# Softmax weights turned through DRAM: one write per block, two read-backs by head, and V of a pair in one transfer

## The chip, the cores and the metric

The kernel runs on one core of one Trainium2 chip. The metric is device time in microseconds (us). The kernel before has a median of 1463.87 us over 3 runs (1461.8 to 1474.76).

## What is computed

The reference is a thresholded attention followed by a bilinear feed-forward layer, all in 32-bit floats.

```python
batch, n_heads, seq, head_dim = (8, 8, 576, 64)
scores = scale * np.matmul(q, k.transpose(0, 1, 3, 2))
thresh = np.max(scores, axis=-1, keepdims=True) - tau
scores = np.where(scores >= thresh, scores, -1000000000.0)
scores = scores - np.max(scores, axis=-1, keepdims=True)
attn = np.exp(scores)
attn = attn / (np.sum(attn, axis=-1, keepdims=True) + 1e-09)
attn_out = np.matmul(attn, v)
# (B,H,S,D) -> (B*S, H*D), then with w_a, w_b (512 x 1536) and w_out (1536 x 512):
a = x @ w_a
b = x @ w_b
return a * b @ w_out
```

## The kernel before, in words

**Tiling.** Heads are taken in pairs (`pairs`, 32 of them, four to a batch). A pair's 576 queries are cut into four blocks of 128 and a tail of 64 (`units`, 160 in all; "block" below means one of them). A tile of weights `tw` has the queries on 128 partitions, and for each of the two heads 576 keys, kept as 18 groups of 32. In a tail both heads share the 128 partitions.

**One step of the main loop** (line 925, step g) issues, in this order: the scores of block g (`scores`, L352, on TensorE, PE); the turn of the weights of block g-1 (`turn_blocks`); the weighing of block g (`weigh`: maximum L359, exp L380, threshold L383); the product with V of a finished half of a pair (`weighted`, which calls `product`, L483); the read-back of block g-2 (`turn_back`); the normalising of block g (L402); loads of q, k and v for pairs some steps ahead (`load` L147, `load_v` L170); stores of finished output rows (L833). Between these, `advance` issues feed-forward matmuls (L633, L706, L763) in portions worked out from column counts, so that PE has other work while weights are prepared.

**The order of the work** is written out by hand: `keep_order` at the end ties every instruction to the one before it on its engine. So each queue does its list strictly in the order written, and an instruction that waits holds up everything behind it on that engine. All transfers of the main loop go through the queue of SyncE (SP). In one step it holds the writes of block g-1 (L457), the read-backs of block g-2 (L466 or L469), then the loads (L147, L170) and the stores.

**How weights are turned.** PV needs the keys on the partitions. VectorE (DVE) transposes each 32 x 32 square in place (L446); what is left is to move 32-partition groups of queries against groups of keys, and that is done through DRAM. `turn_blocks` writes the tile to the DRAM tile `swap` with four transfers, one for each group g of 32 partitions (L457). Each moves 4 pieces of 9 x 32 numbers (1152 bytes) per partition. `turn_back` reads `swap` into the tile `wT` (`turned_tile`, two buffers) with one transfer over 128 partitions (L466), again in pieces of 1152 bytes. For tails, `swap` has two planes, and the read-back of pairs 4 to 31 is two transfers (L469), into the fifth column of the two `wT` tiles of the pair's second half. The first eight blocks (`BY_PE`) are turned by PE instead and don't take this way.

In `wT` the partition is 64 times the head, plus 32 times the half c of the key groups, plus the key's place within its group; slot s (0 to 8) counts the groups in a half. V lies in the same way in `vm`: for pairs 4 to 31 (`HP` is 4) `load_v` issues four transfers, one for each head and half, to 32 partitions each (L170), with rows of 9 x 64 numbers (2304 bytes). Pairs 0 to 3 are loaded twice: at first by head (L172), and a second time (`again`) in the order that the turned weights need.

`product` multiplies slot by slot; within a slot it goes over the heads j, and each matmul reads the 64 partitions of head j:

```python
for s in range(NSLOT):
    for j in range(2):
        rows = slice(j * D, (j + 1) * D)
        for c in range(2):
            y = j ^ c
            nc.tensor.matmul(pv[c * D:(c + 1) * D, y], vm[rows, s], wT[y](rows, s),
```

A half of a pair is two blocks; for pairs 4 to 31 the second half also takes the tail. A block's read-back is issued at step g+2 and the product that uses it is written into step g+3 (`PV_LAG` is 3).

Of the kernel before, what the change touches and what calls it, by code (L numbers as in the profile page):

```python
# [10 lines left out]
FP32 = mybir.dt.float32  # L11
# [41 lines left out]
def kernel(  # L53
# [38 lines left out]
    nc = tc.nc  # L92
    B, H, S, D = q.shape
    P = 128
    Q = 32
    DM = H * D
    DFF = w_a.shape[1]
    HP = H // 2
    NT = 4
# [3 lines left out]
    NB = S // Q  # L103
    R = 96
    NR = S // R
    SH = S // 2
# [3 lines left out]
    NSLOT = 9  # L110
    G = P // Q
# [4 lines left out]
    def pool(name, bufs, **kw):  # L116
        return ctx.enter_context(tc.tile_pool(name=name, bufs=bufs, **kw))
# [5 lines left out]
    scratch = pool("scratch", 3, space=bass.MemoryType.DRAM)  # L123
# [9 lines left out]
    loaded = {}  # L133
# [24 lines left out]
    def load_v(i, again=False):  # L158
        b, hp = pairs[i]
        if not again:  # L160
            loaded[i]["v"] = loads.tile([P, NSLOT, D], FP32, tag="vm", bufs=HP, name="vm")
        for j in range(2):
            rows, half = v[b, 2 * hp + j], loaded[i]["v"][j * D:(j + 1) * D]
            if i >= HP or again:
                if i < HP:
                    rows = rows.rearrange("(c s p) d -> p c s d", c=2, p=Q)
                else:
                    rows = rows.rearrange("(p c s) d -> p c s d", c=2, p=Q)
                for c in range(2):
                    nc.sync.dma_start(half[c * Q:(c + 1) * Q], rows[:, c])  # L170
            else:
                nc.sync.dma_start(half, rows.rearrange("(s p) d -> p s d", p=D))  # L172

# [10 lines left out]
    for f in range(NG):  # L184
        for c in range(HP):
            for dst, w in ((wa_sb, w_a), (wb_sb, w_b)):
                src = []
                for r in range(2):
                    chunks = [(2 * c + e) % HP * 2 + (r + (c >= HP // 2)) % 2 for e in range(2)]
                    cols = slice(f * CW + r * CH, f * CW + (r + 1) * CH)  # L190
                    rows = w[:, cols].bitcast(U32).rearrange("(k p) f -> p k f", p=D)
# [89 lines left out]
    for _ in range(TW_BUFS):  # L281
        t = work.tile([P, 2 * NB, Q], FP32, tag="tw", bufs=TW_BUFS, name="rows")
# [10 lines left out]
    load_rows(2, "k", rooms[5])  # L293
    load_weights(RAWS)
    load_v(0)
    load_rows(3, "q", rooms[6])
    load_rows(3, "k", rooms[7])
# [15 lines left out]
    prepared, scored, weights, turned, whole = {}, {}, {}, {}, {}  # L313
    x_of, xtail_of = {}, {}
    blocks, complete, swaps = [], [], {}
# [97 lines left out]
    def turned_tile():  # L413
        return work.tile([P, G + 1, NSLOT, Q], FP32, tag="wT", bufs=2, name="wT")
# [17 lines left out]
    def part(i, u):  # L432

        if i < HP:
            return {1: (i, 0), 3: (i, 1), NT: (i, 2)}.get(u)
        return {1: (i, 0), NT: (i, 1)}.get(u)
# [4 lines left out]
    def turn_blocks(i, u):  # L441

        ws, _ = weights.pop((i, u))
        t = whole.pop((i, u))
        for w in ws:
            nc.vector.transpose(w, w)  # L446
        if u < NT:
            swap = scratch.tile([G, P, NSLOT * Q], FP32, tag="swap", name="swap")
        else:
            swap = scratch.tile([2, P, NSLOT * Q], FP32, tag="swapt", name="swap")  # L450
        swaps[i, u] = swap
        for g in range(G):
            if u < NT:
                to, n = swap[g], G
            else:
                to, n = swap[g % 2, (1 - g // 2) * D:(2 - g // 2) * D], 2
            nc.sync.dma_start(to.rearrange("(r p) e -> p r e", p=Q),  # L457
                              t[g * Q:(g + 1) * Q, 0:n * NSLOT].rearrange("p (r s) e -> p r (s e)", r=n))

    def turn_back(i, u):  # L460

        swap = swaps.pop((i, u)).rearrange("g p e -> p g e")
        if u < NT or i < HP:
            turned[i, u] = turned_tile()
            n = G if u < NT else 2
            nc.sync.dma_start(turned[i, u][:, 0:n].rearrange("p g s e -> p g (s e)"), swap)  # L466
        else:
            for y in range(2):
                nc.sync.dma_start(turned[i, 2 + y][:, G].rearrange("p s e -> p (s e)"), swap[:, y])  # L469

    def join(out, lo, hi):
        nc.scalar.copy(out, lo)
# [447 lines left out]
    n = 0  # L920
# [4 lines left out]
    for g in range(len(units) + PV_LAG):  # L925
# [4 lines left out]
        if here:  # L930
            i, u = units[g]
# [19 lines left out]
        if g > BY_PE and g <= len(units):  # L951
            turn_blocks(*units[g - 1])
# [14 lines left out]
        if g > BY_PE:  # L967
            advance(PORTIONS[1] * pace)
            n = g - PV_LAG
            if BY_PE <= n < len(units) and part(*units[n]):  # L970
                p, h = part(*units[n])
                if pairs[p][1] == 0:
                    make_x(2 if h == 1 and p >= HP and pairs[p][0] % GT == 0 else 1)
                make_room()
                weighted(*part(*units[n]))
                running["owed"] -= NSLOT * width(*part(*units[n])) // 2
            if BY_PE + 1 < g <= len(units) + 1:
                turn_back(*units[g - 2])
# [20 lines left out]
        for p in range(1, NPR):  # L999
            if g == first[p] - 1:  # L1000
                load_v(p)
        if BY_PE <= g < BY_PE + HP:
            load_v(g - BY_PE, again=True)
# [54 lines left out]
```

## Time and profile before

| | |
|---|---|
| median of 3 runs | 1463.87 us (1461.8 to 1474.76) |
| profiled execution: its time, its span | 1467.37 us, 1465.6 us |
| PE busy | 1387.9 us (95%) |
| DVE, ACT, POOL busy | 1014.9 us (69%), 682.9 us (47%), 479.5 us (33%) |
| chain that ended last: PE, DVE, DMA, SP's queue | 78%, 7%, 5%, 5% |
| SP's transfers (hardware_dynamic q1) | 217.73 MB, 60.7% of 16 engines' span |

The transfers that the change touches, from the list of DMA issues (KB of one, median us from issue to landing) and the tiles' medians of one issue:

| transfer | issues | KB each | us to landing | ns of one issue |
|---|---|---|---|---|
| swap<-tw, block (L457) | 480 | 144 | 2.6 | 433 |
| swap<-tw, tail (L457) | 128 | 72 | 2.0 | 433 |
| wT<-swap, block (L466) | 120 | 576 | 4.7 | 382 |
| wT<-swap, tail of pairs 0 to 3 (L466) | 4 | 288 | 3.3 | 382 |
| wT<-swap, tail of the others (L469) | 56 | 144 | 2.9 | 452 |
| vm<-in_v_dram (L170) | 128 | 72 | 3.3 | 422 |

How to read the lines below: an entry of the waits says which instruction waited (engine, output tile, line of the kernel), for what, how long in total, how often, and the longest. A line of the timeline gives start, duration, engine or queue ("SPq" is SP's queue), line, operation and tiles, and how many instructions are merged. "Issue" in the waits is time in which nothing that the profile shows was waited for. A table by stage gives, for each stretch, the length, then the busy time (and count) of PE, of its weight loads, of DVE, ACT and POOL, then the granted clock, the share of the DMA engines' time, and GB/s.

### The profile page before, as it was taken

To read this page: it belongs to the slowest core of one execution; us is meant where nothing else is said; L and a number is where in the kernel's file an instruction comes from. 1 tells how busy PE (TensorE), PEld (TensorE's weight loads), DVE (VectorE), ACT (ScalarE), POOL (GpSimd) and SP (SyncE) were. 2 spreads that over 40 slices of the span, in tenths; PEclk is the share of its full clock that TensorE was granted. 3 is DMA by queue.
4 is the path that set the end of the run, shared out by engine and by line. 5 is a ranking of instruction groups with operands and counts; after the bars stand their busy time and mean duration, and the time that the engine had idled before them with its cause. 6 is when DMAs were issued, how large, how long until landed. Compare 5 with 4: busy or idle time off the path is not lost.

```text
span 1465.6 us, 76332 instructions
## 1 busy us (share of the span) xinstructions
PE 1387.9 (95%) x34208; PEld 1248.2 (85%) x34208; DVE 1014.9 (69%) x2245; ACT 682.9 (47%) x1243; POOL 479.5 (33%) x668
## 2 busy tenths in 40 slices
PE   5788999999999999999999899999999999999998
PEld 4677687987989889899998788998898979989997
DVE  6898688787767787586757677767767776755223
ACT  5787455545545554454444445444545455431110
POOL 2774713423060606033334224150606060605000
PEclk9999999999999999999999999999999999999999
DMA  9976677668756775577555766477656776450000
GB/s 217 227 207 181 155 183 190 167 169 189 195 135 160 165 203 145 137 174 180 142 135 138 163 165 169 121 177 167 173 147 144 179 188 165 122 148 30 4 17 17
DMA packets 325080, 223.21 MB, mean 152 GB/s; under 512 B 169616, under 2 KB 308880, under 8 KB 324752
## 3 DMA queue, kind: packets, MB, share of 16 engines
q1 hardware_dynamic: 322384, 217.73, 60.7%
q8 instruction: 269, 4.41, 1.3%
q10 hardware_dynamic: 2368, 0.59, 0.2%
q14 instruction: 59, 0.48, 0.1%
HBM read 128.58 MB, written 89.65 MB: 149 GB/s over the span
## 4 chain that ended last, share of the span: by engine, by line
PE 78%; DVE 7%; DMA 5%; SPq 5%; issue 3%; ACT 1%; POOL 1%; ACTq 0%; DVEq 0%; POOLq 0%
PE pab L633 24%; PE pab L706 18%; PE po L763 17%; PE pv L483 9%; PE sc L352 9%; DMA wT<-swap 2%; SPq L457 2%; DVE mx L359 2%; SPq L147 1%; DMA qT<-in_q_dram 1%; DVE tw L446 1%; DVE tw L383 1%; PE po L809 1%; SPq L225 1%; POOL kept L732 0%
## 5 line engine op out<-in xcount | busy, mean ns | idle before, releaser
L402 ACT ACTIVATE tw<-tw,rcp 128x576 f32<-128x576 f32 x272 | 197.8, 769 | 216.9 <-DVE rcp L396 216.8
L359 DVE TENSOR_REDUCE mx<-sc 128x1 f32<-128x576 f32 x288 | 205.6, 751 | 134.6 <-PE sc L352 131.3
L380 ACT ACTIVATE tw<-sc,bias,scalars 128x576 f32<-128x576 f32 x288 | 239.3, 831 | 9.8 <-DMA vm<-in_v_dram 0.2
L599 POOL TENSOR_TENSOR h<-h,u 128x512 f32<-128x512 f32 x28 | 35.1, 1272 | 621.8 <-DVE h L676 485.8
L383 DVE SCALAR_TENSOR_TENSOR tw<-sc,thr,tw 128x576 f32<-128x576 f32 x288 | 223.0, 798 | 14.0 <-ACT tw L380 13.8
L763 PE MATMUL po<-wo_sb,h 64*64 64x256 f32 x3264 | 222.9, 377 | 0.0
L352 PE MATMUL sc<-kT,qT 64*64 64x288 f32 x2016 | 192.0, 405 | 10.5 <-ACT xt L490 4.7
L446 DVE STREAM_TRANSPOSE tw<-tw 128x576 f32<-128x576 f32 x272 | 196.0, 754 | 0.8 <-ACT tw L402 0.8
L483 PE MATMUL pv<-wT,vm 64*64 64x160 f32 (+3 forms) x5184 | 182.4, 275 | 14.3 <-DMA wT<-swap 8.0
L763 PEld LDWEIGHTS po<-wo_sb,h 64*64 64x64 f32 x3264 | 167.4, 133 | 24.9
L483 PEld LDWEIGHTS pv<-wT,vm 64*64 64x64 f32 x5184 | 166.2, 135 | 25.3 <-issue 10.4
L763 PE MATMUL po<-sums_u,h 64*64 64x256 f32 x2448 | 163.9, 376 | 1.6 <-DVE h L714 1.6
L732 POOL TENSOR_TENSOR h<-h 128x256 f32<-128x256 f32 x168 | 117.4, 728 | 114.6 <-PE po L763 100.5
L352 PEld LDWEIGHTS sc<-kT,qT 64*64 64x64 f32 x2016 | 115.1, 133 | 32.5 <-ACT xt L490 12.3
L763 PEld LDWEIGHTS po<-sums_u,h 64*64 64x64 f32 x2448 | 123.4, 133 | 20.7 <-DVE h L714 2.3
L633 PE MATMUL pab<-xU,wb_sb 64*64 64x128 f32 x4096 | 133.5, 270 | 0.2 <-issue 0.2
L379 ACT ACTIVATE bias<-mx,scalars 128x1 f32<-128x1 f32 x288 | 83.0, 288 | 100.6 <-DVE mx L359 100.5
L633 PEld LDWEIGHTS pab<-xU,wb_sb 64*64 64x64 f32 x4096 | 127.6, 133 | 2.6 <-issue 0.5
L491 DVE COPY xT<-pv 64x128 f32<-64x128 f32 (+1 forms) x136 | 38.1, 280 | 120.3 <-PE pv L483 119.1
L633 PE MATMUL pab<-xS,wa_sb 64*64 64x128 f32 x2048 | 110.8, 270 | 3.2 <-POOL xS L506 2.0
L490 ACT COPY xT<-pv 128x128 f32<-128x128 f32 (+1 forms) x68 | 17.6, 258 | 206.0 <-PE pv L483 205.9
L706 PE MATMUL pab<-xS,wb_sb 64*64 64x256 f32 (+1 forms) x1536 | 99.9, 359 | 2.9 <-issue 2.9
(137 smaller groups left out, 2429.0 us busy)
## 6 DMA issues: line engine op xcount, KB each, us to landing
swap<-tw SPq DMA_DIRECT2D x480, 144.0 KB, 2.6
wT<-swap SPq DMA_DIRECT2D x120, 576.0 KB, 4.7
vm<-in_v_dram SPq DMA_DIRECT2D x128, 72.0 KB, 3.3
swap<-tw SPq DMA_DIRECT2D x128, 72.0 KB, 2.0
kT<-in_k_dram SPq DMA_DIRECT2D x112, 72.0 KB, 4.3
wT<-swap SPq DMA_DIRECT2D x56, 144.0 KB, 2.9
out_dram<-kept SPq DMA_DIRECT2D x30, 256.0 KB, 4.0
qT<-in_q_dram SPq DMA_DIRECT2D x112, 40.0 KB, 4.5
```

The lines of the kernel that those rows point to most:

```text
L352: nc.tensor.matmul(sc[j if u < NT else 0][to, c], qT[r, q0:q0 + D], kT[r, c * SH:(c + 1) * SH], start=True, stop=True)
L359: nc.vector.tensor_reduce(mx[:, c], sc[j], axis=AX.XY, op=ALU.max)
L379: nc.scalar.activation(bias[:, j:j + 1], mx[:, j:j + 1], AF.Copy, scale=e_nscale)
L380: nc.scalar.activation(wb[j], sb[j], AF.Exp, bias=bias[:, j:j + 1], scale=e_scale)
L383: nc.vector.scalar_tensor_tensor(out=wv, in0=sb[j], scalar=thr[:, j:j + 1], in1=wv, op0=ALU.is_ge, op1=ALU.mult, accum_out=sums[:, j:j + 1])
L402: nc.scalar.activation(w, w, AF.Copy, scale=rcp[:, j:j + 1])
L446: nc.vector.transpose(w, w)
L483: nc.tensor.matmul(pv[c * D:(c + 1) * D, y], vm[rows, s], wT[y](rows, s), start=(s == 0), stop=(s == NSLOT - 1))
L633: nc.tensor.matmul(out[c * D:(c + 1) * D, r, f * P:(f + 1) * P], w[g][k][rows, w0:w0 + D], moving[k][rows], start=(fresh and k == 0 and f ...
L706: nc.tensor.matmul(pab[c * D:(c + 1) * D, r], w[rows, f // n, k, fs + c * D:fs + (c + 1) * D], moving, start=(k == 0), stop=(k == H - 1))
L732: (nc.vector if state["over"] else nc.gpsimd).tensor_tensor(*a, **kw)
L763: nc.tensor.matmul(po[c * D:(c + 1) * D, r, y], ht[rows, t0:t0 + D], other[rows, f], start=(f == 0), stop=(f == NF // 2 - 1))
```

## The change

Three things change, and nothing else.

1. `turn_blocks` writes a block in one transfer: 128 partitions, for each head one run of 576 numbers (2304 bytes). `swap` is now one plane of [128, 576] for each head; a tail is one plane.
2. `turn_back` reads back by head: for each head j one transfer to the 64 partitions of that head, in pieces of 288 numbers (1152 bytes). Two consecutive pieces of a DRAM row go to two neighbouring partitions. A tail of pairs 4 to 31 takes four transfers (two heads, two tiles), one of pairs 0 to 3 takes two.
3. The half c of the key groups is now the lowest bit of the partition and no longer its bit of value 32. So V of a pair, for pairs 4 to 31, is one transfer to 128 partitions with rows of 2304 bytes. The second load of pairs 0 to 3 still takes four transfers, now to every second partition.

```diff
@@ load_v
+        vm = loaded[i]["v"]
+        if i >= HP:
+            nc.sync.dma_start(vm, v[b, 2 * hp:2 * hp + 2].rearrange("j (p s) d -> (j p) s d", s=NSLOT))
+            return
         for j in range(2):
-            rows, half = v[b, 2 * hp + j], loaded[i]["v"][j * D:(j + 1) * D]
-            if i >= HP or again:
-                if i < HP:
-                    rows = rows.rearrange("(c s p) d -> p c s d", c=2, p=Q)
-                else:
-                    rows = rows.rearrange("(p c s) d -> p c s d", c=2, p=Q)
+            rows, half = v[b, 2 * hp + j], vm[j * D:(j + 1) * D]
+            if again:
                 for c in range(2):
-                    nc.sync.dma_start(half[c * Q:(c + 1) * Q], rows[:, c])
+                    nc.sync.dma_start(half[c::2], rows[c * SH:(c + 1) * SH].rearrange("(s p) d -> p s d", p=Q))
@@ turn_blocks
-        if u < NT:
-            swap = scratch.tile([G, P, NSLOT * Q], FP32, tag="swap", name="swap")
-        else:
-            swap = scratch.tile([2, P, NSLOT * Q], FP32, tag="swapt", name="swap")
+        n = len(ws)
+        swap = scratch.tile([n, P, 2 * NSLOT * Q], FP32, tag="swap" if n == 2 else "swapt", name="swap")
         swaps[i, u] = swap
-        for g in range(G):
-            if u < NT:
-                to, n = swap[g], G
-            else:
-                to, n = swap[g % 2, (1 - g // 2) * D:(2 - g // 2) * D], 2
-            nc.sync.dma_start(to.rearrange("(r p) e -> p r e", p=Q),
-                              t[g * Q:(g + 1) * Q, 0:n * NSLOT].rearrange("p (r s) e -> p r (s e)", r=n))
+        nc.sync.dma_start(swap.rearrange("j p e -> p j e"), t[:, 0:n * NB].rearrange("p (j n) e -> p j (n e)", j=n))
@@ turn_back
-        swap = swaps.pop((i, u)).rearrange("g p e -> p g e")
+        swap = swaps.pop((i, u))
         if u < NT or i < HP:
             turned[i, u] = turned_tile()
-            n = G if u < NT else 2
-            nc.sync.dma_start(turned[i, u][:, 0:n].rearrange("p g s e -> p g (s e)"), swap)
-        else:
+        for j in range(2):
+            rows = slice(j * D, (j + 1) * D)
+            if u < NT:
+                nc.sync.dma_start(turned[i, u][rows, 0:G].rearrange("p g s e -> p g (s e)"),
+                                  swap[j].rearrange("(g p) (c e) -> (p c) g e", g=G, c=2))
+                continue
+            back = swap[0, (1 - j) * D:(2 - j) * D].rearrange("(y p) (c e) -> (p c) y e", y=2, c=2)
+            if i < HP:
+                nc.sync.dma_start(turned[i, u][rows, 0:2].rearrange("p y s e -> p y (s e)"), back)
+                continue
             for y in range(2):
-                nc.sync.dma_start(turned[i, 2 + y][:, G].rearrange("p s e -> p (s e)"), swap[:, y])
+                nc.sync.dma_start(turned[i, 2 + y][rows, G].rearrange("p s e -> p (s e)"), back[:, y])
```

## The prediction

> **What bounds the kernel now.** First the stage table, for where TensorE (PE) has holes, since a change of transfers can win no more than those. Columns: stretch, length, busy time of each engine, granted clock, DMA share, GB/s.
>
> ```profile
> 0.00:120.00 120.00, 85.33 (x2148) 72.88 (x2152) 95.34 (x213) 83.86 (x170) 64.96 (x80) 0.96 0.95 223
> 120.00:1320.00 1200.00, 1162.76 (x28537) 1046.49 (x28533) 868.10 (x1940) 583.73 (x1048) 392.80 (x554) 1.00 0.66 162
> 1320.00:1440.00 120.00, 119.97 (x3180) 112.40 (x3176) 40.48 (x68) 13.16 (x22) 21.69 (x34) 1.00 0.04 14
> ```
>
> PE is idle for 37.2 us of the 1200 in which the changed transfers run (120 to 1320). After that PE is full with feed-forward work left over, so the end comes when PE has done its list: a microsecond of PE idle filled before 1320 brings the end forward by one, and a new one puts it back. The first 120 us use the changed path little: blocks 0 to 7 are turned on PE.
>
> Second, PE's waits in 120 to 1320: waited for, us in total, times, longest.
>
> ```profile
> PE pv L483 <- DMA wT<-swap: 8.0, 6, 2.7
> PE pab L633 <- issue: 7.8, 14, 1.9
> PE sc L352 <- ACT xt L490: 4.7, 4, 1.2
> PE sc L352 <- DVE xt L491: 3.2, 3, 1.1
> PE pv L483 <- issue: 2.6, 4, 1.0
> ```
>
> The largest named wait is the product with V (L483) for turned weights read back from DRAM: 8.0 us. So the changed path ends last only at a few places; elsewhere PE does not wait for it.
>
> Third, the queue of SyncE (SP) at one such place, and the chain of waits there.
>
> ```profile
> 205.45 3.74 SPq L457 DMA_DIRECT2D swap<-tw  x4
> 209.29 0.40 SPq L466 DMA_DIRECT2D wT<-swap  x1
> 209.79 2.08 SPq L147 DMA_DIRECT2D qT<-in_q_dram  x4
> 211.91 2.88 SPq L170 DMA_DIRECT2D vm<-in_v_dram  x4
> ...
> 209.29 5.17 DMA wT<-swap
> 214.46 0.04 issue
> 214.50 2.08 PE pv L483 x67
> ```
>
> The read-back of block g-2 stands in SP's queue behind the four writes of block g-1. They took 3.74 us to issue; without a hold-up they take 1.76. From the trace's landing records I paired 65 PV blocks with the last read-back each uses: in 8 it lands after PV has begun (6.5 us together), in 26 less than 1.0 us before PV or later, in 34 less than 1.5. That list prices a shift: every read-back landing 0.5 us sooner fills 3.5 us, 1.0 sooner 5.2, 1.5 sooner 6.5; 0.5 later opens 5.5 us, 1.0 later 15.0, 1.5 later 30.8.
>
> Fourth, the rate of each transfer when it is alone: a read-back (704.0 to 705.4) and the four writes of a block (707.9 to 709.6); the last columns are DMA share and GB/s.
>
> ```profile
> 704.00:705.40 1.40, 1.40 (x32) 1.40 (x28) 1.37 (x2) 1.08 (x3) 0.00 (x0) 1.00 0.93 329
> 707.90:709.60 1.70, 1.70 (x72) 1.70 (x65) 1.16 (x5) 0.47 (x1) 0.00 (x0) 1.00 0.96 216
> ```
>
> Same bytes, same 1152-byte pieces, DMA engines over 90% busy in both: 329 GB/s for one transfer over 128 partitions, 216 for four over 32 each.
>
> **What the Trainium skill says.** "SBUF — State Buffer", Door 1: The DMA port swizzle: the DMA side has 16 ports, partitions 0 to 31 reach 8, 0 to 63 the same 8, and only a transfer over all 128 reaches 16. The trace agrees for 32 against 128 (216 against 329 GB/s); it shows no large 64-partition transfer, so for those I rest on the page. "DMA: Bandwidth & Descriptors", Rules for kernel authors: two transfers to disjoint partition halves serialize. No run yet shows that; the change makes just such a pair. [...] Here a read-back with the queue to itself took 4.1 us to land, against 1.8 for 590 kB at 329 GB/s.
>
> **The change, part by part.**
>
> *Writes.* A block of two heads: four transfers of 144 KB become one of 576 KB over 128 partitions, in rows of 2304 bytes. 120 such blocks and 32 tails: 608 issues become 152. Issue by the tile's median (0.433 us): 1.76 us become about 0.45, so SP is free 1.3 us sooner. Moving time: 590 kB at 216 is 2.73 us; at 329 it is 1.80. The bounds are 1.80 and 2.73 (writes to DRAM need not run like reads); I take 1.80 on the port page. Nobody waits for a write itself: its reader is issued one step, about 8 us, later, against a landing of 2.6 us. It counts only as what fills the rings ahead of the read-back.
>
> *Read-backs.* One of 576 KB becomes two of 288 KB over 64 partitions: 124 + 56 issues become 248 + 112. Each further issue costs 0.38 to 0.45 us of SP. Moving time: 1.80 us at 329 becomes 2.73 at 216, if 64 partitions are as 32; bounds 1.80 and 2.73. PV alternates heads from one matmul to the next, so an early first half is worth nothing. PV now waits for two landings per tile and head pair in place of one; queued behind it on PE is everything, in written order.
>
> *The sum at a critical block*, from the place at 707: before, writes issued from 707.00, read-back issued at 708.92, landed 4.8 us later at 713.7. After: bytes flow about 1.0 us after the first issue (as at 707), writes 1.80, read-backs straight behind in the same rings (issued by 708.3, long before 709.8) 2.73, receipt about 0.6 (bytes of the lone read-back end at 705.4, its landing is at 706.0): 707.0 + 1.0 + 1.80 + 2.73 + 0.6 = 713.1. That is 0.6 us sooner. With both bounds good (1.80, 1.80) 1.5 sooner; with both bad (2.73, 2.73) 0.3 later. Where issues were held up, as at 209 (3.74 in place of 1.76), a further 1 to 2 us come, and these are the places where PE waits. By the list above, 0.6 sooner everywhere is 3.8 us, and with the hold-ups some 5; one fifth I take off, because a PE that starts PV sooner meets its next wait sooner (scores waiting for the PSUM copies, 4.7 + 3.2 us). **-4 us.**
>
> *Tails.* Four writes of 72 KB become one; two read-backs become four for 28 tails and one becomes two for 4. Last issue: 1.75 + 0.45 = 2.2 us after the start of the block's writes before, 0.45 + 3 x 0.45 = 1.8 after. 295 kB in halves: 1.4 us at 216 in place of 0.9. Together +0.1 us, nothing to the list.
>
> *V.* 28 pairs go from four transfers over 32 partitions to one over 128 (row length 2304 bytes as before), 84 issues x 0.422 = 35 us of SP off. It hides under SP's slack except where q, k and v come together (157 to 232, 302 to 378): there a v group holds SP for 1.8 to 3.8 us, and the next block's writes stand behind it. Between 0 and -3 us; I take -0.5, since most of it is in the hold-ups already counted. The four pairs whose V is loaded again keep four transfers each, only to every second partition: 0. K's order of keys within a row, the matmuls and their operands' sizes stay as they are: 0; their order in every queue is written out (the order of each engine is fixed at the end), so no work changes place.
>
> *Sum:* the profiled execution took 1467.37 us (span 1465.6); minus 4.5 it would be 1462.9. It lies 3.5 us above the median of the runs, 1463.87; from that median, **1459.4 us**.
>
> **Rivals.**
> *Hidden or given back.* PE's idle time at PV is filled but returns at the next scores or in the copies of PV's banks: -2 to +2 us, 1464. For: PE's other waits sum to more than this one. Against: after 1320 PE has no waits at all, so idle filled anywhere counts.
> *The half-port read-back takes the place of the issue wait (slower).* Place: PV behind L466. If the pair of halves needs more than it saves, landings come later, and more than half of all blocks have under 1.5 us to spare. It decides at 1.0 us later (15 us, 1%): writes and read-backs would have to need 6.1 us together in place of the 4.5 of my sum, which is writes no faster than now and read-backs at 175 GB/s. At 1.5 us later it is +31, some 1494; at 1.2 later about 1485. For: the skill's pages both speak against halves. Against: 216 GB/s is measured for transfers with as few ports, and the earlier issue is arithmetic.
> *SP's queue was worth more than PE's waits show (faster by over 1%).* The chain gives SP's queue 5% and wT's transfers 2%; with 360 fewer issues q, k and blocks all come sooner. It must fill 15 of the 37 us idle: about 1447. Against: of those 37 us only some 13 name a transfer or stand at PV.
> That the transfers do not become fewer or wider is excluded by the access patterns; how wide the rows are on the wire is not.
>
> **How the numbers follow.** Forecast 0.55 (own range 1455 to 1463), hidden 0.20, half-port 0.15, SP's queue 0.10. 1% is about what a measurement of this kernel can tell from no change; bounds 1449.2 and 1478.5. Faster 0.10 (the last rival), same 0.75 (forecast and hidden), slower 0.15. Range 1448 to 1477: both middle cases, the near part of each outer one.
>
> **What would show it.** Right: writes landing near 3.5 us at 0.4 us of issue; GB/s near 329 in them; halves near 216; the wait of PV for wT below 4 us. Wrong: that wait above 10 us, halves landing later than 6 us behind the writes' first issue, or a time outside the range with PE's idle time in 120 to 1320 unchanged.

## The result, and the profile after

The changed kernel takes 1478.2 us (median of 17 runs, 1471.76 to 1483.28), the kernel before, in the same comparison, 1467.05 us (17 runs, 1461.67 to 1474.76). The ratio is 1.007, interval 1.0052 to 1.0089: slower by 0.7%, where 1459.4 us was forecast, and about 1 us above the upper end of the range. The profiled execution of the changed kernel took 1477.18 us (span 1475.4), 9.8 us more span than before.

First the stage table of the changed kernel, in the columns of the one shown for before.

```profile
120.00:1320.00 1200.00, 1158.17 (x28333) 1046.29 (x28329) 866.83 (x1936) 582.48 (x1046) 392.90 (x554) 1.00 0.62 161
1320.00:1440.00 120.00, 118.38 (x3159) 99.54 (x3156) 40.84 (x69) 13.94 (x23) 21.70 (x34) 1.00 0.10 27
```

In 120 to 1320 PE is idle for 41.8 us instead of 37.2, and it gets through 204 matmuls fewer. Next, PE's waits in that stretch: waited for, us in total, times, longest.

```profile
PE pab L632 <- issue: 16.0, 19, 1.8
PE sc L352 <- ACT xt L489: 7.0, 6, 1.3
PE pab L705 <- issue: 3.5, 5, 1.3
PE pv L482 <- issue: 2.1, 3, 0.8
...
PE pv L482 <- DMA wT<-swap: 1.5, 2, 0.8
```

The wait of the product with V (PV) for turned weights fell from 8.0 to 1.5 us, as forecast. But the wait at the top has no name: 16.0 us of "issue" ahead of the first layer of the feed-forward (`pab`, L632, L633 before), where it was 7.8. The two rows of `pab` together hold 19.5 us.

The summed time from each matmul's start to the next, after 120 us and put down to the kind of the later one, shows what the waits alone do not (us, worked out from the start times in the trace):

| | `pab` | PV | scores | second layer | span |
|---|---|---|---|---|---|
| before | 705.2 | 162.3 | 144.1 | 327.7 | 1465.6 |
| after | 724.9 | 152.5 | 143.6 | 328.2 | 1475.4 |

PV gained 9.8 us; `pab`, which no edit touches and whose data no changed transfer carries, lost 19.7. The sum is the change of the span. So the question was not why the gain at PV failed to come, but what holds PE in the feed-forward.

The transfers themselves did what was forecast. The page's list of DMA issues (count, size, median us from issue to landing), and the queue of SyncE (SP) at the place shown for before at 205:

```profile
swap<-tw SPq DMA_DIRECT2D x120, 576.0 KB, 3.5
wT<-swap SPq DMA_DIRECT2D x240, 288.0 KB, 4.6
```

```profile
207.73 0.56 SPq L450 DMA_DIRECT2D swap<-tw  x1
208.39 1.51 SPq L460 DMA_DIRECT2D wT<-swap  x2
```

The write's issue takes 0.56 us there, where four held SP for 3.74. The rates of the write alone (702.7 to 704.4) and of the two half read-backs (708.8 to 711.2), in the last column:

```profile
702.70:704.40 1.70, 1.67 (x62) 1.43 (x56) 1.70 (x4) 0.00 (x0) 0.00 (x0) 1.00 0.91 343
708.80:711.20 2.40, 2.40 (x51) 2.40 (x45) 2.07 (x4) 2.08 (x5) 0.00 (x0) 1.00 0.95 234
```

**What else uses the DMA engines.** The page's list of queues has a second row, the same in both kernels:

```profile
q8 instruction: 269, 4.41, 1.3%
```

These are 269 packets of 16 KB. PE's 34208 matmuls and as many weight loads are 68416 instructions; divided by 256 that is 267. So they are PE's own instructions, one packet for every 256. "Runtime: NRT & Kernel Launch" of the Trainium skill, section Instruction fetch mechanics, says just this: an engine's instructions are streamed in 16 KiB blocks of 256 through a DMA queue of the sequencer. It adds that crossing a block is mostly hidden. The trace agrees on the block, not on "hidden". One place in the changed kernel, in order: PE's timeline, SP's timeline, and the DMA queues in 899.0 to 901.7.

```profile
899.99 0.40 PE L632 MATMUL pab<-xT,wa_sb 64*64 64x128 f32 x8
900.21 0.40 PE L632 MATMUL pab<-xS,wa_sb 64*64 64x128 f32 x8
901.69 0.38 PE L632 MATMUL pab<-xS,wa_sb 64*64 64x128 f32 x5 [1.08 <-issue]
```

```profile
899.04 0.38 SPq L450 DMA_DIRECT2D swap<-tw  x1
899.52 2.09 SPq L460 DMA_DIRECT2D wT<-swap  x2
```

```profile
q1 hardware_dynamic: 1091, 0.67, 90.8%
q8 instruction: 1, 0.02, 3.2%
```

PE stops in the middle of a run of equal matmuls. A write and two half read-backs have just been issued, data holds the engines for 90.8% of the window, and in it lies one instruction packet, which ended 1.27 us before PE went on. In these lines 8 matmuls take 0.22 us; with as many weight loads, a block of 256 instructions lasts some 3.5 us at that rate (an estimate), while 2.66 us passed from the start of this fetch until PE went on. To count such places I took PE's stalls (over 0.25 us from start to start, after 120 us) that end 1.1 to 1.75 us after the end of an instruction packet: 30 with 22.4 us before, 39 with 36.4 us after. Within `pab` they are 13.0 and 30.3 us; that is 17.3 of the 19.7 lost. Some of these are coincidence: windows of the same width at other distances hold 2.5 to 10.2 us.

A count by place leaves chance nearly out. If the fetch causes a stall, the stall must come at a fixed place in PE's stream. Number all of PE's records in the trace (matmuls, weight loads and those of its sequencer; 68897 before, 269.1 blocks of 256). Of the 104 stalls before, 21 end at the places 193 to 195 of a block, and 35 of the 120 after, where chance would put one or two. They hold 15.4 us before and 32.8 after, in `pab` 12.9 and 30.0; all other stalls in `pab` hold 9.4 and 10.5. So 17.1 of the 19.7 us stand at one place in the instruction stream, whatever the matmul there reads. Below, these are the stalls "at the seam".

How late a fetch starts, against its place in the stream (one every 256 instructions, the earliest of each run taken as zero): median 1.27 us before, 1.61 after; one in ten over 2.66 before, over 3.53 after.

### The profile page after: what moved, and what is told of

Read it like the earlier page. It is cut to its first block, busy times and chain, and to the rows that moved or that the text cites. A ratio compares the mean times of both kernels' runs of the same rounds, so it can differ in the third digit from the quotient of the medians.

```text
span 1475.4 us, 75468 instructions
## 1 busy us (share of the span) xinstructions
PE 1390.5 (94%) x34208; PEld 1240.3 (84%) x34208; DVE 1017.0 (69%) x2245; ACT 682.8 (46%) x1243; POOL 480.2 (33%) x668
## 4 chain that ended last, share of the span: by engine, by line
PE 84%; DVE 8%; issue 4%; DMA 2%; ACT 1%; POOL 1%; SPq 0%; DVEq 0%; ACTq 0%; POOLq 0%
PE pab L632 27%; PE po L762 19%; PE pab L705 18%; PE sc L352 10%; PE pv L482 9%; DVE mx L359 2%; DVE tw L383 1%; PE po L808 1%; DVE tw L446 1%; DMA wT<-swap 1%; POOL kept L731 1%; DVE low L260 0%; PE tp L427 0%; DVE xT L490 0%; DMA scalars<-in_tau_dram 0%
## 5 line engine op out<-in xcount | busy, mean ns | idle before, releaser
L383 DVE SCALAR_TENSOR_TENSOR tw<-sc,thr,tw 128x576 f32<-128x576 f32 x288 | 223.3, 798 | 15.0 <-ACT tw L380 14.7
L762 PE MATMUL po<-wo_sb,h 64*64 64x256 f32 x3264 | 218.4, 377 | 0.0
L352 PE MATMUL sc<-kT,qT 64*64 64x288 f32 x2016 | 192.1, 404 | 10.2 <-ACT xt L489 7.0
L762 PEld LDWEIGHTS po<-wo_sb,h 64*64 64x64 f32 x3264 | 163.3, 133 | 26.4
L482 PEld LDWEIGHTS pv<-wT,vm 64*64 64x64 f32 x5184 | 165.2, 134 | 16.8 <-issue 10.4
L762 PE MATMUL po<-sums_u,h 64*64 64x256 f32 x2448 | 160.9, 376 | 1.6 <-DVE h L713 1.6
L632 PE MATMUL pab<-xU,wb_sb 64*64 64x128 f32 x4096 | 133.2, 270 | 1.0 <-issue 1.0
L632 PEld LDWEIGHTS pab<-xU,wb_sb 64*64 64x64 f32 x4096 | 126.8, 133 | 4.5 <-issue 1.5
L632 PE MATMUL pab<-xS,wa_sb 64*64 64x128 f32 x2048 | 108.5, 271 | 5.9 <-issue 3.8
L489 ACT COPY xT<-pv 128x128 f32<-128x128 f32 (+1 forms) x68 | 17.6, 259 | 198.6 <-PE pv L482 198.6
```

Of the source, the lines that this page charges most:

```text
L352: nc.tensor.matmul(sc[j if u < NT else 0][to, c], qT[r, q0:q0 + D], kT[r, c * SH:(c + 1) * SH], start=True, stop=True)
L383: nc.vector.scalar_tensor_tensor(out=wv, in0=sb[j], scalar=thr[:, j:j + 1], in1=wv, op0=ALU.is_ge, op1=ALU.mult, accum_out=sums[:, j:j + 1])
L632: nc.tensor.matmul(out[c * D:(c + 1) * D, r, f * P:(f + 1) * P], w[g][k][rows, w0:w0 + D], moving[k][rows], start=(fresh and k == 0 and f ...
L762: nc.tensor.matmul(po[c * D:(c + 1) * D, r, y], ht[rows, t0:t0 + D], other[rows, f], start=(f == 0), stop=(f == NF // 2 - 1))
```

## The experiments

Theories. **Ports**: the halves, at 64 partitions, move at a lower rate and come late at PV (the rival of the forecast). **SP**: the longer or more frequent issues hold something up. **Fetch**: long transfers keep the DMA engines from PE's next instructions. The expectations use letters, and call `pab` feed-forward. H, W and V name the part of the change that keeps the fetches waiting: the half read-backs, the one long write, or V with the longer rows. L says that a transfer does it by its length; D that the bytes ahead of the fetch do it, however they are cut. P stands in `e7` for the ports, against I for the second transfer; from `e12` on it stands for read-backs that arrive sooner, and so a PE that comes sooner to its next fetch, however long the transfers are. Each ratio is to the kernel before, run on the same chip, with its 95% interval. Columns of the tables: `pab` and PV as above; "issue" is PE's wait at L632 or its counterpart; "late" is the mean delay of a fetch. These columns come from one profiled execution of each kernel, and executions of the kernel before lie up to 13 us apart (1461.67 to 1474.76), so a few microseconds in them decide nothing; nor do one or two tenths in "late", whose zero is each run's own.

### One part at a time

`e1_v_and_rows`: the kernel before with V in one transfer and the DRAM tile in rows of 2304 bytes; still four writes over 32 partitions and one read-back over 128.

```diff
-            swap = scratch.tile([G, P, NSLOT * Q], ...)
+            swap = scratch.tile([G, 2, Q, 2 * NSLOT * Q], ...)
...
+            nc.sync.dma_start(to, t[g * Q:(g + 1) * Q, 0:n * NB].rearrange("p (j n) e -> p j (n e)", j=n))
...
+        swap = swaps.pop((i, u)).rearrange("g j p (c e) -> (j p c) g e", c=2)
```

> V of a pair in one transfer and rows of 2304 bytes stay; the write is again four transfers of 32 partitions and the read-back again one of 128. Theory H (two half read-backs hold up the instruction fetches of PE: in the changed kernel they begin 1.61 us after their place in the stream in the median, against 1.27 before, and 39 stalls of PE end just behind a fetch, against 30): ratio to before 0.995 to 1.002, fetch stalls as before. Theory W (the one long write holds them up): the same, 0.995 to 1.002. Theory V (the one transfer of V, or the longer rows, hold them up): 1.004 to 1.009.

`e2_write_in_four`: the changed kernel with its write cut in four by partitions.

```diff
+        for g in range(G):
+            r = slice(g * Q, (g + 1) * Q)
+            nc.sync.dma_start(swap[:, r].rearrange("j p e -> p j e"), t[r, 0:n * NB].rearrange("p (j n) e -> p j (n e)", j=n))
```

> The changed kernel with the write of a block in four transfers of 32 partitions again; read-backs by head and V in one stay. H: still slow, 1.007 to 1.015 (PV's wait for wT comes back on top, 8 us or more). W: fetch stalls back to about 30, ratio 1.000 to 1.006 with PV's wait for wT at 8 to 15 us.

`e3_before_halves`: the kernel before, its read-back cut in two by head (tails too).

```diff
+            for j in range(2):
+                r = slice(j * D, (j + 1) * D)
+                nc.sync.dma_start(turned[i, u][r, 0:n].rearrange("p g s e -> p g (s e)"), swap[r])
```

> The kernel before with each read-back cut into two transfers of 64 partitions, nothing else. H: fetch stalls up to about 40 and PV's wait above 8 us, ratio 1.007 to 1.018. W and V: fetch stalls as before, PV's wait 8 to 15 us, ratio 1.000 to 1.006.

`e4_v_in_four`: the changed kernel with V of pairs 4 to 31 in four transfers.

```diff
+            for j in range(2):
+                for c in range(2):
+                    nc.sync.dma_start(vm[j * D + c:(j + 1) * D:2], v[b, 2 * hp + j].rearrange("(p c s) d -> p c s d", c=2, p=Q)[:, c])
```

> The changed kernel with V of a pair in four transfers of 32 partitions again. V: back to 1.000 to 1.003. H and W: stays at 1.005 to 1.010.

| | ratio | `pab` | PV | issue | late |
|---|---|---|---|---|---|
| before | | 705.2 | 162.3 | 7.8 | 1.42 |
| after | 1.007 (1.0052 to 1.0089) | 724.9 | 152.5 | 16.0 | 1.75 |
| `e1_v_and_rows` | 0.9979 (0.9967 to 0.9992) | 703.6 | 155.2 | 8.8 | 1.39 |
| `e2_write_in_four` | 1.0094 (1.0071 to 1.0117) | 705.1 | 170.7 | 7.3 | 1.44 |
| `e3_before_halves` | 1.0259 (1.0228 to 1.029) | 704.4 | 197.7 | 11.1 | 1.59 |
| `e4_v_in_four` | 1.0102 (1.0081 to 1.0122) | 720.7 | 156.6 | 14.7 | 1.72 |

PE's waits in `e2_write_in_four`, and then the same rows in `e3_before_halves`:

```profile
PE pv L484 <- DMA wT<-swap: 10.2, 13, 1.7
PE pab L634 <- issue: 7.3, 12, 1.2
```

```profile
PE pv L487 <- DMA wT<-swap: 24.6, 28, 3.3
PE pab L637 <- issue: 11.1, 13, 1.8
```

From `e1` to `e2` the read-backs become halves (and the planes of the DRAM tile with them): +1.1%, nearly all of it at PV (155.2 to 170.7). From `e2` to the changed kernel only the four writes become one: PV wins 18.2 us, and `pab` loses 19.8. So the halves cost about the same either way; with the one write in front the cost stands elsewhere. V and the long rows are worth 0.2%. Neither H nor W fits alone: `e2` has the ratio that H named and the `pab` that W needs, and `e3` lies above both ranges.

### Halves or simply two transfers; one write or four

`e7_before_two_wide` and `e8_before_four_wide`: the kernel before, its read-back cut in two or in four by columns, each over 128 partitions.

```diff
+            for g in range(0, n, n // 2):
+                r = slice(g, g + n // 2)
+                nc.sync.dma_start(turned[i, u][:, r].rearrange("p g s e -> p g (s e)"), swap[:, r])
```

> The kernel before with each read-back of a block cut in two by columns, both over 128 partitions: as many read-backs as in the run with two halves of 64 partitions (1.026)[...]. Tails keep one or two read-backs. Theory P (ports[...]): close to before, 0.999 to 1.006. Theory I (the second transfer and its landing cost it): 1.015 or more.

> The kernel before with each read-back of a block in four transfers of 128 partitions, 144 KB each. L: the fetches of instructions come sooner than in the kernel before (start 1.1 us or less behind their place in the median, in place of 1.27), feed-forward up to 10 us shorter, PV longer by 5 to 15 us because of three more issues: 0.997 to 1.006. D: feed-forward as before, PV longer: 1.004 to 1.012.

`e5_write_in_two` and `e6_write_in_four_wide`: the changed kernel, its write cut in two by head, or in four by head and half row, over 128 partitions each time.

```diff
+        for j in range(n):
+            nc.sync.dma_start(swap[j], t[:, j * NB:(j + 1) * NB].rearrange("p n e -> p (n e)"))
```

> The changed kernel with the write of a block in two transfers, one for each head, both over all 128 partitions. Theory L (a long transfer holds up a fetch of instructions in proportion to what it puts on one DMA engine at a time): fetch stalls between the two, feed-forward about 10 us less than in the changed kernel, PV as there: ratio to before 0.997 to 1.003. Theory D (it is the closeness of write and read-backs, the number of bytes that stand ahead of the fetch, and not how they are cut): nothing changes, 1.006 to 1.011.

> The same in four transfers of 144 KB, each over all 128 partitions with rows of 1152 bytes: as many issues as before the change, and as small per engine[...]. L: feed-forward back to the kernel before (20 us less than changed), PV between: 0.996 to 1.003. D: 1.005 to 1.012, since the issues cost PV some of its gain.

| | ratio | `pab` | PV | issue | late |
|---|---|---|---|---|---|
| `e7_before_two_wide` | 0.9996 (0.9976 to 1.0016) | 705.4 | 167.0 | 6.7 | 1.38 |
| `e8_before_four_wide` | 1.0103 (1.0068 to 1.0137) | 690.5 | 191.3 | 1.3 | 1.23 |
| `e5_write_in_two` | 1.0049 (1.0031 to 1.0068) | 720.3 | 152.0 | 16.6 | 1.62 |
| `e6_write_in_four_wide` | 1.0069 (1.0047 to 1.0091) | 712.7 | 165.2 | 12.3 | 1.50 |

Two wide read-backs cost nothing where two halves cost 2.6% (`e3`): behind four writes it is the half width, not a second transfer as such. The width brings two things, though: the lower rate, and a longer issue (0.62 us each in `e3`, 0.47 in `e7`, medians); `e3` cuts the tails as well. And `e8` was the surprise that set the rest of the study. PE's waits in it:

```profile
PE pv L484 <- DMA wT<-swap: 15.6, 12, 2.9
PE pab L634 <- issue: 1.3, 3, 0.7
```

The same bytes in four short transfers come later at PV, but the nameless wait is almost gone, and `pab` falls to 690.5 us, 14.7 below before. Shorter writes in the changed kernel do the same by steps: 724.9 in one, 720.3 in two, 712.7 in four wide, 705.1 in four over 32 partitions (`e2`). In the last two PV also gets later, so these four do not yet part a shorter write from a later read-back. The ratios did not settle it either: `e5` lies between the ranges of L and D, and `e6` and `e8` in that of D, though their `pab` fell.

### Read-backs early, so that PV does not wait

To take PV out of the comparison, the read-back of block g-2 is issued ahead of the writes of block g-1, wherever no product of the same step still needs the buffer: on `e1` (`e9_early_read`), on the changed kernel (`e11_changed_early_read`) and on `e2` (`e12_write_in_four_early_read`).

```diff
+        behind = BY_PE <= g - PV_LAG < len(units) and part(*units[g - PV_LAG])
+        if BY_PE + 1 < g <= len(units) + 1 and not behind:
+            turn_back(*units[g - 2])
...
-            if BY_PE + 1 < g <= len(units) + 1:
+            if BY_PE + 1 < g <= len(units) + 1 and behind:
```

> As the run that keeps only V in one transfer and the longer rows (0.998), and a read-back that doesn't have to wait for a product with V of the same step is issued ahead of the writes of the next block, not behind them. The order on PE is the same. PV's wait for wT under 1 us, PV 2 to 5 us shorter, feed-forward as there: 0.993 to 0.998.

> The changed kernel with the same read-backs ahead of the next block's write. D (the fetch stands behind write and read-backs that follow each other in the rings): they are now some microseconds apart for most blocks, so feed-forward falls by 10 us or more from the changed kernel: 0.995 to 1.001. L (the write's own length): feed-forward stays 15 to 20 us over the kernel before: 1.004 to 1.010.

> The changed kernel with four short writes of 32 partitions and with the read-backs ahead of the next block's writes: PE as punctual at PV as in the changed kernel (PV 148 to 153 us after 120 us), writes as short as before. L: feed-forward 703 to 712 us, ratio 0.994 to 1.001. P: feed-forward 718 to 728 us, ratio 1.002 to 1.010.

`e15_early_read_in_two` and `e10_early_read_in_four` are `e9` with its read-back cut by columns in two and in four, by the same lines as in `e7` and `e8`.

> As the run with early read-backs (1.002; feed-forward 717.9, PV 148.2 us), each read-back of a block in two transfers of 128 partitions; in four it was 0.991 (699.1, 156.1). Length of the read-backs (L): feed-forward between, 704 to 713, PV 148 to 153: 0.993 to 0.999. Only arriving sooner (P): feed-forward 714 to 722, ratio 1.000 to 1.005.

> The same with the read-back of a block in four transfers of 128 partitions (144 KB each). Theory L (a transfer holds up an instruction fetch by its own length on an engine): waits of PE for nothing shown, at L633, fall to about 1 us as in the run of the kernel before with four read-backs, feed-forward 10 to 15 us shorter than before; the three more issues now fall into PV's slack, PV at most 10 us longer than with one: 0.984 to 0.995. Were the shorter feed-forward of that earlier run only the other side of its longer waits at PV, feed-forward stays at 703 to 705: 0.995 to 1.004.

| | ratio | `pab` | PV | issue | late |
|---|---|---|---|---|---|
| `e9_early_read` | 1.002 (1.0007 to 1.0033) | 717.9 | 148.2 | 13.5 | 1.50 |
| `e15_early_read_in_two` | 0.9941 (0.9922 to 0.996) | 710.4 | 149.9 | 11.4 | 1.39 |
| `e10_early_read_in_four` | 0.9909 (0.9884 to 0.9934) | 699.1 | 156.1 | 2.7 | 1.26 |
| `e11_changed_early_read` | 1.0087 (1.0063 to 1.0112) | 728.8 | 150.4 | 16.4 | 1.77 |
| `e12_write_in_four_early_read` | 1.0035 (1.0018 to 1.0052) | 718.4 | 150.3 | 15.9 | 1.55 |

My expectation for `e9` failed: PV lost its wait (0.5 us left), and yet the kernel came out slower than `e1`, because `pab` rose by 14.3 us. A punctual read-back is thus no gain as long as it is one long transfer. Cut in two and in four, still early, it gives back 7.5 and 18.8 us in `pab`, while PV takes back 1.7 and 7.9; the ratio falls by 0.8% and 1.1%. That is the dose that the fetch theory asks for, and SP has more issues in it, not fewer. `e11` against `e12` is the write alone at an equal PV (150.4, 150.3): one long write costs `pab` 10.4 us, and by the ratios the kernel 0.5% (the profiled execution of `e11` was 7 us above its median, so the ratios are the safer figure). But `e12` itself came out in the range of P, not of L: with short writes and a PE that waits little at PV, `pab` is 718.4 us, 13.3 above `e2`. So the punctual read-back adds to the loss beside the long write.

### A write that nobody needs

Added to `e1`: from step 60 on each step issues one more write of 576 KB from the constant first-layer weights to a DRAM tile that nothing reads; in one transfer (`e13_extra_long_write`) or in four of 144 KB (`e14_extra_short_writes`, whose lines are shown).

```diff
+        if 60 <= g < len(units):
+            spare = scratch.tile([4, P, NSLOT * Q], FP32, tag="spare", name="spare")
...
+            for c in range(4):
+                nc.sync.dma_start(spare[c], some[:, c])
```

> The kernel with V in one transfer and longer rows (0.998), and in each step from the 60th on a useless write more of 576 KB over 128 partitions, in one transfer, to a place that nobody reads. L: its fetches start later (mean 1.6 us or more behind their place against 1.39), feed-forward 10 us or more longer than in the next run. P: fetches and feed-forward as in the next run, within 4 us.

> The same bytes in the same pieces in four transfers of 144 KB over 128 partitions. L: fetches start about as in the kernel without them (1.4 to 1.5 us), feed-forward 703 to 710 us; PV 0 to 15 us longer for the four more issues in SP's queue. P: as the run before.

Long: ratio 1.0201 (1.0164 to 1.0239), `pab` 738.9, PV 160.6, fetches 2.10 us late in the mean. Short: 1.0359 (1.0329 to 1.0389), `pab` 720.0, PV 195.0, fetches 1.83 us late. PE's waits with the long write, then with the short ones:

```profile
PE pab L633 <- issue: 26.9, 21, 3.0
PE pv L483 <- DMA wT<-swap: 6.8, 6, 2.1
```

```profile
PE pv L483 <- DMA wT<-swap: 29.5, 15, 6.7
PE pab L633 <- issue: 14.5, 14, 3.0
```

A useless transfer with no reader raises `pab` by 35.3 us over `e1` (703.6), so data dependences are not the way by which a write reaches the feed-forward. Equal bytes in short pieces raise it by 16.4, which L had not expected (703 to 710 us). In the total the order is the reverse: the short ones cost more, because they made PV late. So this pair shows that a transfer without a reader reaches the feed-forward; it does not show cleanly what its length does, since a PE that waits at PV also gives a fetch time.

### The changed kernel with short read-backs

Now each half read-back in two transfers of 144 KB, on `e11` (`e16_changed_early_read_cut`) and on the changed kernel itself, at the original place (`e17_changed_cut`). Bytes, partitions, the one long write and its issue stay; SP gets two issues more for each block.

```diff
-                nc.sync.dma_start(turned[i, u][rows, 0:G].rearrange("p g s e -> p g (s e)"),
-                                  swap[j].rearrange("(g p) (c e) -> (p c) g e", g=G, c=2))
+                for g in range(0, G, 2):
+                    nc.sync.dma_start(turned[i, u][rows, g:g + 2].rearrange("p g s e -> p g (s e)"),
+                                      swap[j, g * Q:(g + 2) * Q].rearrange("(g p) (c e) -> (p c) g e", g=2, c=2))
```

> The changed kernel with early read-backs (1.009; feed-forward 728.8, PV 150.4 us), each half read-back of a block in two transfers of 144 KB. L: feed-forward 708 to 720, ratio 0.997 to 1.004; the long write is left. P: feed-forward 724 to 732, ratio 1.006 to 1.012.

> The changed kernel (1.007; feed-forward 724.9, PV 152.5 us) with each half read-back of a block in two transfers of 144 KB, at its own place. Length of the read-backs as the cause: waits of PE for nothing shown at L633 below 4 us, feed-forward 694 to 706; two more issues (0.9 us) in front of PV cost 8 to 16 us by the list of the prediction: 0.996 to 1.002. Otherwise feed-forward 718 or more, and 1.009 to 1.016.

| | ratio | `pab` | PV | late | stalls behind a fetch: all, in `pab` |
|---|---|---|---|---|---|
| after | 1.007 (1.0052 to 1.0089) | 724.9 | 152.5 | 1.75 | 36.4, 30.3 |
| `e17_changed_cut` | 0.9961 (0.9948 to 0.9974) | 692.9 | 164.3 | 1.21 | 15.4, 8.5 |
| `e11_changed_early_read` | 1.0087 (1.0063 to 1.0112) | 728.8 | 150.4 | 1.77 | |
| `e16_changed_early_read_cut` | 0.9907 (0.9889 to 0.9926) | 696.1 | 157.0 | 1.20 | 17.6, 5.7 |

PE's waits in `e17_changed_cut`, then in `e16_changed_early_read_cut`:

```profile
PE pv L483 <- DMA wT<-swap: 8.9, 11, 1.6
...
PE pab L633 <- issue: 2.7, 4, 1.7
```

```profile
PE pv L483 <- DMA wT<-swap: 3.6, 5, 1.5
...
PE pab L633 <- issue: 1.3, 1, 1.3
```

Twice the read-back issues, more waiting at PV, and the kernel is faster: 1458.02 us in the median for `e17`. The nameless wait fell from 16.0 to 2.7 us and `pab` by 32.0 us. Of these, 21.8 lie in the stalls behind a fetch (30.3 to 8.5), and 24.9 at the seam (30.0 to 5.1); some 7 us have no account. `e16` fell below its ranges: the long write is left, and hardly any of the loss. `e16`, median 1451.59 us, beats both kernels, as does `e10` (1452.08); their intervals do not tell them apart.

A later PV could also have given the fetches time. It is not what removes the stalls here: PV is later in `e2` (170.7) and `e3` (197.7) than in `e17` (164.3), and both keep more of them. Taken together, with `pab` split into its stalls at the seam and the rest:

| | `pab` | at the seam | rest |
|---|---|---|---|
| before | 705.2 | 12.9 | 692.3 |
| after | 724.9 | 30.0 | 694.9 |
| `e2_write_in_four` | 705.1 | 15.1 | 690.0 |
| `e3_before_halves` | 704.4 | 19.6 | 684.8 |
| `e8_before_four_wide` | 690.5 | 3.6 | 686.9 |
| `e9_early_read` | 717.9 | 19.7 | 698.2 |
| `e12_write_in_four_early_read` | 718.4 | 24.3 | 694.1 |
| `e11_changed_early_read` | 728.8 | 30.7 | 698.1 |
| `e13_extra_long_write` | 738.9 | 43.4 | 695.5 |
| `e17_changed_cut` | 692.9 | 5.1 | 687.8 |
| `e16_changed_early_read_cut` | 696.1 | 3.5 | 692.6 |

`pab` spans 48 us over these runs, the rest 13. `e11` also speaks against D: its read-backs are issued 5.9 us after the last write in the median, in place of 2.0, and the stalls at the seam are as in the changed kernel (30.7 and 30.0).

## Why the prediction was wrong

- **Writes**: right. The issue at 899 takes 0.38 us, the landing 3.5 us as named, the rate 343 GB/s against 329 forecast. That a write has no waiting reader was right too; that it therefore costs nothing was not (`e11` against `e12`: 10.4 us in `pab`).
- **Read-backs**: rate right (234 GB/s against 216), so what the forecast took from "SBUF — State Buffer", Door 1, of the Trainium skill, that 64 partitions are no faster than 32, agrees within 8% (216 was measured in writes, 234 in reads); and the pair together stayed below the 329 of one wide transfer, so the halves did not add up. The issue was under-priced: 0.61 us each in the median (1.51 for the two at 208), where 0.38 to 0.45 was forecast.
- **The sum at a critical block**: right in sign, too small in size. The forecast filled 4 us; the wait for `wT` fell by 6.5, and PV's time by 9.8.
- **V**: small, as forecast; 0.2% together with the long rows, and the price of undoing it (`e4`) lies at the edge of the intervals.
- **The step that failed** is in the sum: every term was a shift of landings turned into PE's wait for `wT`, and all else on PE was taken to stand still ("so no work changes place"; "idle filled anywhere counts"). The order of PE's work did stay; the arrival of its instructions did not. They come over the same DMA engines, were in no term, and `pab` lost 19.7 us. -9.8 at PV and +19.7 in `pab` make +9.9; the span grew by 9.8. All four signs that the forecast named for being right came true (3.5 us, 343 GB/s, 234 GB/s, a wait of 1.5 us); none of them looks at PE outside PV. PE's waits before held the hint: 7.8 us of "issue", the second largest wait, that I listed and did not ask after.
- **Rivals**: the half-port rival had the sign, for the wrong reason as it stood. Its place was PV, and PV got faster. It is true of halves behind four writes (`e2`, `e3`). That the half rate acts on the fetches in the changed kernel is not shown: with early read-backs behind four writes, one of full width (`e9`) and two halves (`e12`) leave `pab` equal, 717.9 and 718.4. "SP's queue was worth more" is refuted: `e17` has 240 issues more and is faster. "Given back" was nearest in kind, but named the next scores or copies; scores stayed at 144 us.

What is shown: the loss stands at one place in PE's instruction stream, and cutting the read-backs, with bytes and width kept, removes it. Not separated is what in the cut does it. Four issues of 0.61 us (median in `e17`) take SP 2.4 us, about as long as the bytes take to move (2.5 us for 590 kB at 234 GB/s), so a cut also keeps SP from running ahead of the engines; no run hands over short transfers at once or long ones slowly. What is only argued: how the engines choose between the two queues. "DMA: Bandwidth & Descriptors", Queues, rings and completion order, says that each engine alternates between queues packet by packet; no record here shows the turns inside an engine, so whether the fetch stands behind one long packet or behind several stays open. Open too is why an early read-back, whole or in halves, raises `pab` even with short writes (`e9`, `e12`); shorter transfers cure it (`e10`, `e15`), but whether it is the transfer's place or the more punctual PE that brings it there was not separated.

## What to carry to other kernels

When PE is near full with small matmuls, its instruction stream is a client of the DMA engines with a deadline of its own: look for "issue" waits in the middle of a run of equal matmuls, and price a longer transfer by them even if nobody waits for its data. "DMA: Bandwidth & Descriptors", Rules for kernel authors, asks for few large transfers; here read-backs in pieces of 144 KB beat those of 288 (`e17` against the changed kernel, 1.1%) and of 576 (`e10` against `e9`, 1.1%), as long as they came in time for PV (not in `e8`). Compare the time between starts for each kind of matmul, not the waits alone: what leaves one kind may come back in another.

## What I had not expected of the hardware

- PE's fetches take 1.3% of the DMA engines' time in both kernels, and the stalls at their seam sum to 15.4 us before and 32.8 us after.
- The time of the first feed-forward layer, 690.5 to 738.9 us over the runs, varies mostly by the stalls at that one place in the instruction stream: without them it is 685 to 698 us.
- Where a transfer of 576 KB is issued once more in each of 100 steps, with no reader, PE's nameless wait in `pab` triples (8.8 to 26.9 us) and the kernel slows by 2.2% against `e1` (1.0201 over 0.9979).
- Two read-backs in place of one are free if each spans 128 partitions (0.9996) and cost 2.6% if each spans 64 (1.0259).
